# Full-width state products in the first unit of a gated linear-attention kernel, and one output product of the third unit placed in front of the fifth unit's logarithms

## The chip, the cores and the metric

The kernel runs on one core of a Trainium2 chip. The core has a matrix engine (PE, with its weight loads shown as PEld), a vector engine (DVE), a scalar engine (ACT), a general engine (POOL) and an engine that only issues transfers (SP). Each of them works through its own list of instructions in order, and they wait for one another through semaphores. The metric is the device time of one execution in microseconds (us), the median of several runs.

## The reference

A gated recurrence over 4 batches of 8 heads, 768 tokens and head size 48 is followed by a feed-forward block with the ELU function. All in float32:

```python
mag = np.sqrt(a_re * a_re + a_im * a_im)
scale = np.minimum(mag, 0.999) / (mag + 1e-06)
a_re_n, a_im_n = (a_re * scale, a_im * scale)
for t in range(S):
    ar, ai = (a_re_n[:, :, t, :, None], a_im_n[:, :, t, :, None])
    new_re = ar * S_re - ai * S_im
    new_im = ar * S_im + ai * S_re
    kv = np.einsum('bhd,bhe->bhde', k[:, :, t], v[:, :, t])
    S_re, S_im = (new_re + kv, new_im)
    y[:, :, t] = np.einsum('bhd,bhde->bhe', q[:, :, t], S_re)
...
x = np.ascontiguousarray(attn_out.transpose(0, 2, 1, 3)).reshape(B * S, H * D)
h = x @ w_in
g = np.where(h > 0.0, h, alpha * (np.exp(np.minimum(h, 0.0)) - 1.0))
return (g @ w_out).astype(np.float32)
```

The feed-forward block has 3072 tokens, width 384 and inner width 2048.

## The kernel before

**Units.** The work is cut into 12 units, numbered from 0. A unit is one stretch of 128 tokens of two sequences (two of the four batches), so 256 tokens. Units 0 and 1 hold the first 128 tokens of the two pairs of sequences, units 2 and 3 the next 128, and so on. Inside a unit the index n picks the sequence, and each stretch of 128 tokens is treated as two chunks of 64 (index c).

**Decays.** The recurrence is unrolled with logarithms and angles. For units 2 and later a unit's chain is: squares of the gate's parts on ACT (`squares`, L709 and L710), their sum (`joined`, L716, on DVE for units 0 to 2 and on POOL after), two logarithms on ACT (`logarithms`, L735 and L736), two exponentials on ACT (`powers`, L746 and L747), then `lengths` (L772, DVE), `ratios` (L759 and L760, POOL), `slopes` (L780, DVE), `angles` (L815, ACT), the sums of logarithms on PE (`quartered`, L883, which reads the result of `lengths`), exponentials (L893, ACT), the sums of angles on PE (`turned`, L832), sines and cosines (`waves`, ACT), and the scaled and gated keys and queries. Squares, logarithms, exponentials and sines lie in different ACT function tables, and a change of table is an instruction of its own.

**Attention of a unit.** `transposed` turns the gated keys and queries (L1003, copied out of PSUM by ACT at L1004). `scores` makes the 64x64 products inside each chunk (L1011), masked by DVE at L1016. `states` multiplies gated keys and values into the state's increment (L1035) and DVE updates the state S (L1044 where there is no state yet, else L1046, then L1048). `values` makes the outputs from scores (L1058) and from the state (L1065); ACT copies them out (L1073, L1077), and `seam` moves some rows by DMA (L1090) so that they form the input x of the feed-forward block.

In `states` the 128 rows of a stretch are two chunks of 64 rows, each with its own accumulator tile g. The gated keys of a head have two parts (real and imaginary, index i), each padded from 48 to 64 columns:

```python
        for h in range(H):
            for c, g in enumerate(gs):
                for i in range(2):
                    nc.tensor.matmul(
                        g[ts(i, HP), h], lhsT=gates["k"][ts(c, L), n, h, i],
                        rhs=vn[u % 2][ts(c, L), n, ts(h, D)], start=True, stop=True,
                    )
```

So each of these products uses a 64x64 quarter of the PE array: 8 heads x 2 chunks x 2 parts = 32 products for one n.

**Feed-forward of a unit.** `inner` multiplies x with w_in (L1110), `elu` applies the function (ACT L1119 and L1120, DVE L1121) into g. For units 0 and 1 `project` multiplies with w_out (L1131). From unit 2 on the second product is made as a Winograd-like scheme of seven products of half size: DVE forms sums and differences of g (`folded`, L1194) and of w_out (`combined`, L1174, once), and `product(u, k, h)` for k = 1 to 7 and two halves h multiplies them (L1216). `product(u, 1, 1)` ends with an ACT copy of the first product (L1224) into a tile named ee; `product(u, 6, ...)` writes the other half of the same PSUM tile. DVE and ACT finish the outputs (L1228, L1235, L1237, L1241), and SP stores them (L1238).

**Order.** Nothing schedules these steps for the kernel: the order in which the steps are called is the order of each engine's instructions. A list written out by hand, `first` (L1352 to L1411), comes first; it also holds the conversion of the weights from 64-bit to 32-bit floats (`convert`, DVE L40 to L50 and L653), cut into pieces between the other steps. All later steps are put in a plan with a due time each (`put`, `decays_of`, `gates_of`, `values_of`, `layer_of`, L1412 to L1436), and those that are not in `first` already follow in the order of their due times:

```python
    items = [(fn, tuple(args)) for fn, *args in first]
    items += [x[2:] for x in sorted(plan, key=lambda x: x[:2]) if x[2:] not in items]
```

Of the kernel before, what the change touches and what calls it, by code (L numbers as in the profile page):

```python
# [17 lines left out]
L = 64  # L18
# [50 lines left out]
HP = 64  # L69
# [436 lines left out]
def kernel(  # L506
# [13 lines left out]
    B, H, S, D = q.shape  # L520
# [38 lines left out]
    vn = [cst.tile([C, NB, HD + G], FP32, name=f"vn{n}") for n in range(2)]  # L559
    gates = {key: cst.tile([C, NB, H, 2, HP], FP32, name=key + "g") for key in ("k", "q")}  # L560
# [10 lines left out]
    def work(shape, tag="w"):  # L571
        return ps.tile(shape, FP32, tag=tag, bufs=3, name=tag)
# [4 lines left out]
    def where(u):  # L577
        return u % (B // NB) * NB, u // (B // NB) * C
# [114 lines left out]
    def new(tag, bufs=1, shape=None):  # L693
        return sb.tile(shape or [C, NB, H, D], FP32, tag=tag, bufs=bufs, name=tag)
# [325 lines left out]
    def states(u, n):  # L1020

        x = nat[u]
        b, s = where(u)
        x["S", n] = [state.get(b + n)]
        if s == S - C:
            last = C // L - 1
        else:
            last = C // L
        gs = [
            work([C, H, D], "w" if u else "mlp") for c in range(last)  # L1030
        ]
        for h in range(H):
            for c, g in enumerate(gs):
                for i in range(2):
                    nc.tensor.matmul(  # L1035
                        g[ts(i, HP), h], lhsT=gates["k"][ts(c, L), n, h, i],
                        rhs=vn[u % 2][ts(c, L), n, ts(h, D)], start=True, stop=True,
                    )
        for c, g in enumerate(gs):
            old = x["S", n][-1]  # L1040
            new_s = new("S", 8, [C, H, D])
            wide = x["T"][:, n, c].unsqueeze(2).to_broadcast([C, H, D])
            if old is None:
                nc.vector.tensor_tensor(out=new_s, in0=g, in1=wide, op=ALU.mult)  # L1044
            else:
                nc.vector.tensor_tensor(out=new_s, in0=g, in1=old, op=ALU.add)  # L1046
                eng = nc.vector if u < 2 else nc.gpsimd
                eng.tensor_tensor(out=new_s, in0=new_s, in1=wide, op=ALU.mult)  # L1048
            x["S", n].append(new_s)
        state[b + n] = x["S", n][-1]  # L1050
# [253 lines left out]
    parts = [("in", m) for m in range(NF // 2)] + [("out", m) for m in range(NF // WF)]  # L1304
# [39 lines left out]
    def values_of(u, *at):  # L1344
        fns = (transposed, "q"), (transposed, "k"), (scores,), (states,), (values,)
        for n in range(NB):
            for x, (fn, *key) in zip(at[5 * n :], fns):
                put(x, fn, u, *key, n)
        put(at[-1], seam, u)
# [14 lines left out]
        (transposed, 0, "k", 0), (transposed, 0, "q", 1), (carry_on, 0), (transposed, 0, "q", 0),  # L1364
        *4 * [(convert,)], (scores, 0, 0), (transposed, 0, "k", 1), (scores, 0, 1), (load_a, 1),
        (squares, 1), (joined, 1), (fetch, "in", 3), (logarithms, 1), (states, 0, 0),
        (values, 0, 0), (powers, 1), (convert,), (states, 0, 1), (lengths, 1), (load_qk, 1),
        (convert,), (ratios, 1), (values, 0, 1), (seam, 0), (warm, 2), (warm, 2), (decays, 1),
        (load_a, 2), (warm, 1), (inner, 0, 0), *2 * [(convert,)], (noted, 1), (scaled, 1),
# [37 lines left out]
        (scores, 3, 0), (inner, 2, 8), (elu, 2, 6), (combined, 3, 0), (inner, 2, 10), (noted, 3),  # L1407
        (elu, 2, 8), (elu, 2, 10), (combined, 3, 1), (transposed, 3, "q", 1), (values, 3, 0),
        (inner, 2, 12), (transposed, 3, "k", 1), (states, 3, 1), (elu, 2, 12), (scores, 3, 1),
        (inner, 2, 14), (elu, 2, 14), (values, 3, 1), (folded, 2, 0),  # L1410
    ]  # L1411
    def layer_of(u, at_h, at_p):  # L1412
        for m in range(NF // 2):
# [64 lines left out]
```

## Time and profile before

| what | value |
|---|---|
| median of 5 runs | 705.52 us |
| the five runs | 702.76, 704.08, 705.52, 705.54, 705.6 us |
| the profiled execution, device time | 703.02 us |
| its span, first to last instruction | 701.3 us |
| PE busy | 671.9 us (96%), 6720 matmul records |
| PE weight loads busy | 577.4 us (82%) |
| DVE, ACT, POOL busy | 388.7, 398.9, 197.5 us |
| mean granted PE clock | 0.991 of full speed |
| instruction queue of PE (q8) | 55 packets, 0.90 MB |

Times in the profile are microseconds from the start of the span. A product in float32 appears as two weight loads and two matmul records. In a line of the timeline, the numbers are start and length in us, then the engine, the line of the kernel, the operation, what is written and read, and how many records were merged; a bracket gives the idle time of the engine just before, and what ended it. In a line of the waits, the numbers are total us, times and the longest. Lengths of matmul records overlap, since matmuls are pipelined.

### The profile page before, as it was taken

The numbers are of one execution on the slowest core, as the hardware profiler recorded it, in microseconds if no ns is written. First come the engines' busy times: TensorE is split into PE (matmuls) and PEld (weight loads), VectorE is DVE, ScalarE is ACT, GpSimd is POOL, SyncE is SP. The second block draws the span as 40 slices with busy tenths as digits, with TensorE's granted clock in tenths as the row PEclk, the third lists the DMA queues.
The fourth block names the chain that finished last, engine by engine and source line by source line (L and its number), as shares of the span: only waits on it lengthen the run. The fifth ranks groups of instructions, "written<-read, shape, count | busy, mean of one in ns | idle before, by whom it ended". The sixth has DMA issues, their size and how long they took to land.

```text
span 701.3 us, 15900 instructions
## 1 busy us (share of the span) xinstructions
PE 671.9 (96%) x6720; PEld 577.4 (82%) x6720; DVE 388.7 (55%) x579; ACT 398.9 (57%) x630; POOL 197.5 (28%) x207
## 2 busy tenths in 40 slices
PE   8798899988998999999999999999999999999996
PEld 6677776566787888888988989889888988989995
DVE  5989999713955554554553553553554643642151
ACT  6865445658563765755656656657557547641230
POOL 2000000125413414415415405405407305402000
PEclk9999999999999999999999999999999999999999
DMA  9976646062062821921821831731741531100001
GB/s 165 188 146 109 152 140 175 6 110 53 5 133 63 134 51 41 141 41 52 125 60 53 122 60 53 113 70 53 109 74 53 113 70 53 47 1 7 23 0 29
DMA packets 149900, 56.00 MB, mean 80 GB/s; under 512 B 129172, under 2 KB 142652, under 8 KB 149820
## 3 DMA queue, kind: packets, MB, share of 16 engines
q1 hardware_dynamic: 146240, 53.53, 39.9%
q0 software_dynamic: 3360, 1.22, 1.4%
q8 instruction: 55, 0.90, 0.6%
q14 instruction: 25, 0.20, 0.1%
q10 hardware_dynamic: 220, 0.14, 0.1%
HBM read 48.88 MB, written 4.78 MB: 77 GB/s over the span
## 4 chain that ended last, share of the span: by engine, by line
PE 81%; DVE 6%; SPq 3%; DMA 3%; ACT 3%; issue 2%; POOL 1%; DVEq 0%; ACTq 0%; POOLq 0%
PE mlp L1110 30%; PE mlp L1216 26%; PE w L1003 5%; PE mlp L1131 4%; PE w L1011 3%; PE w L1035 3%; PE y L1065 3%; SPq L596 2%; PE y L1058 2%; DMA w<-in_moe_w_in_dram 2%; PE w L832 2%; PE w L1131 1%; PE w L883 1%; DVE wf L43 1%; DVE g L1121 1%
## 5 line engine op out<-in xcount | busy, mean ns | idle before, releaser
L1110 PE MATMUL mlp<-x,w_in 128*128 128x256 f32 x1152 | 261.9, 381 | 2.3 <-DVE g L1121 1.0
L1110 PEld LDWEIGHTS mlp<-x,w_in 128*128 128x128 f32 x1152 | 214.4, 190 | 32.4 <-DVE g L1121 1.8
L1119 ACT ACTIVATE ee<-mlp 128x512 f32<-128x512 f32 x96 | 57.3, 597 | 129.9 <-PE mlp L1110 120.4
L1121 DVE SCALAR_TENSOR_TENSOR g<-ee,mlp 128x512 f32<-128x512 f32 x96 | 65.4, 684 | 118.0 <-ACT ee L1120 110.7
L1216 PE MATMUL mlp<-w_out,g 128*128 128x192 f32 x640 | 111.3, 328 | 0.0
L1216 PEld LDWEIGHTS mlp<-w_out,g 128*128 128x128 f32 x640 | 104.3, 190 | 2.8
L1048 POOL TENSOR_TENSOR S<-S,T 128x384 f32<-128x384 f32 x36 | 29.8, 829 | 165.6 <-DVE S L1046 165.6
L1120 ACT ACTIVATE ee<-ee 128x512 f32<-128x512 f32 x96 | 60.5, 631 | 2.8
L1216 PE MATMUL mlp<-w,g 128*128 128x192 f32 x320 | 58.0, 337 | 2.9 <-ACT ee L1224 2.9
L1216 PEld LDWEIGHTS mlp<-w,g 128*128 128x128 f32 x320 | 52.6, 193 | 8.8 <-issue 5.0
L1194 DVE TENSOR_TENSOR g<-g 128x512 f32<-128x512 f32 x80 | 56.8, 710 | 2.7
L856 POOL DMA_DIRECT2D carry<-n x10 | 5.0, 499 | 144.7 <-DVE n L840 144.7
L1046 DVE TENSOR_TENSOR S<-w,S 128x384 f32<-128x384 f32 x38 | 21.1, 555 | 40.8 <-PE w L1035 25.5
L988 POOL TENSOR_TENSOR kg<-k,cs 128x1536 f32<-128x1536 f32 x9 | 38.9, 4322 | 16.3 <-issue 16.3
L1090 POOL DMA_DIRECT2D x<-y x65 | 31.7, 495 | 41.6 <-ACT y L1077 41.6
L893 ACT ACTIVATE n<-w 64x384 f32<-64x384 f32 (+1 forms) x60 | 28.1, 486 | 26.8 <-PE w L883 26.1
L1235 ACT COPY o<-mlp 128x192 f32<-128x192 f32 x10 | 3.2, 318 | 62.8 <-DMA out_dram<-o 52.9
L716 POOL TENSOR_TENSOR n<-n 128x768 f32<-128x768 f32 x9 | 16.3, 1816 | 66.9 <-ACT n L710 66.9
L1131 PE MATMUL mlp<-w_out,g 128*128 128x384 f32 x96 | 32.9, 490 | 1.6 <-DVE g L1121 1.6
L1004 ACT COPY qt<-w 128x512 f32<-128x512 f32 x48 | 25.4, 584 | 12.0 <-PE w L1003 12.0
L1011 PEld LDWEIGHTS w<-qt,kt 128*64 128x64 f32 x768 | 24.5, 137 | 7.9 <-issue 4.5
L1216 PE MATMUL mlp<-wt,g 128*128 128x192 f32 x160 | 30.1, 331 | 0.0
(165 smaller groups left out, 977.4 us busy)
## 6 DMA issues: line engine op xcount, KB each, us to landing
w<-in_moe_w_out_dram SPq DMA_DIRECT2D x8, 768.0 KB
g<-in_moe_w_in_dram SPq DMA_DIRECT2D x16, 384.0 KB
g<-in_moe_w_out_dram SPq DMA_DIRECT2D x16, 384.0 KB
w<-in_moe_w_in_dram SPq DMA_DIRECT2D x16, 288.0 KB
vn<-in_v_dram SPq DMA_DIRECT2D x24, 192.0 KB
out_dram<-o SPq DMA_DIRECT2D x48, 96.0 KB
ar<-in_a_re_dram SPq DMA_DIRECT2D x22, 192.0 KB
ai<-in_a_im_dram SPq DMA_DIRECT2D x22, 192.0 KB
```

Source lines behind the costliest of these rows:

```text
L988: eng.tensor_tensor(out=to[:, :, :, 0:D], in0=each.unsqueeze(2).to_broadcast([C, step * H, 2, D]), in1=x["cs"][:, n * H : (n + step) * H], ...
L1003: nc.tensor.transpose(t[:, h], of, ident)
L1011: nc.tensor.matmul(t[ts(c, L), h], lhsT=x["kt", n][:, h, ts(c, L)], rhs=x["qt", n][:, h, ts(c, L)], start=True, stop=True,)
L1048: eng.tensor_tensor(out=new_s, in0=new_s, in1=wide, op=ALU.mult)
L1090: eng.dma_start(out=x["x"][ds(j * HP + D, G), i], in_=x["y"][ds(j * HP + i * G, G)])
L1110: nc.tensor.matmul(t[:, e], lhsT=w_in[:, i, ts(f + e, C)], rhs=x["x"][:, i], start=(i == 0), stop=(i == NI - 1),)
L1119: nc.scalar.activation(out=e, in_=t, func=AF.Relu, scale=-1.0)
L1120: nc.scalar.activation(out=e, in_=e, func=AF.Exp, scale=-1.0)
L1121: nc.vector.scalar_tensor_tensor(out=x["g", f // 8][:, f % 8 : f % 8 + 2], in0=e, scalar=-1.0, in1=t, op0=ALU.add, op1=ALU.max)
L1131: nc.tensor.matmul(x["o", n], lhsT=x["g", f // 8][:, f % 8, ts(n, C)], rhs=w_out[:, f], start=(f == 0), stop=(f == NF - 1),)
L1194: nc.vector.tensor_tensor(out=S_of(u, k, h), in0=a, in1=b, op=op)
L1216: nc.tensor.matmul(to, lhsT=a[:, m], rhs=b[:, m], start=(first and h == 0 and m == 0), stop=False, skip_group_check=True,)
```

## The change

In `states`, for unit 0 only, the two parts of a head's keys are taken as one weight of 128 columns, and the product writes all 128 partitions of the accumulator at once. All other units keep the two parts. In the list `first`, eight entries are added, among them `(product, 2, 1, 1)`, directly behind `(product, 2, 1, 0)` and in front of `(product, 2, 4, 0)`, `(logarithms, 4)` and `(powers, 4)`.

```diff
         for h in range(H):
             for c, g in enumerate(gs):
-                for i in range(2):
+                k = gates["k"][ts(c, L), n, h]
+                parts = [(g[ts(i, HP), h], k[:, i]) for i in range(2)]
+                if u == 0:
+                    parts = [(g[:, h], k.rearrange("p i d -> p (i d)"))]
+                for to, of in parts:
                     nc.tensor.matmul(
-                        g[ts(i, HP), h], lhsT=gates["k"][ts(c, L), n, h, i],
-                        rhs=vn[u % 2][ts(c, L), n, ts(h, D)], start=True, stop=True,
+                        to, lhsT=of, rhs=vn[u % 2][ts(c, L), n, ts(h, D)], start=True, stop=True,
                     )
...
-        (inner, 2, 14), (elu, 2, 14), (values, 3, 1), (folded, 2, 0),
+        (load_a, 4), (inner, 2, 14), (elu, 2, 14), (values, 3, 1), (folded, 2, 0),
+        (begun, 4), (squares, 4), (joined, 4), (product, 2, 1, 0), (product, 2, 1, 1),
+        (product, 2, 4, 0), (logarithms, 4), (powers, 4),
```

In the instruction lists of the two kernels this comes to three differences. On PE, the two groups of 32 products 64x48 of unit 0 become two groups of 16 products 128x48. On PE, the 16 products that followed `values` of unit 3 stood as 4 of k=1, 4 of k=4, 4 of k=1, 4 of k=4 and now stand as 8 of k=1 and 8 of k=4. On ACT, the copy L1224 of unit 2 stood behind the two logarithms and the two exponentials of unit 4 with their two table changes, and now stands behind the two squares and in front of the first table change. The lists of DVE, POOL and SP are the same in both, so no transfer moves.

## The prediction

> **What bounds the kernel.** The page comes first: PE is busy for 671.9 of 701.3 us, and in the chain of work that ended last it holds 81%. So a change counts where PE stands still, or where something else sets PE's pace. The waits of PE from 110 us on name the largest stop:
>
> ```profile
> engine line waited for: us in total, times, longest us
> PE mlp L1216 <- ACT ee L1224: 2.9, 1, 2.9
> PE w L1003 <- POOL kg L988: 1.4, 1, 1.4
> PE w L883 <- DVE n L772: 1.3, 1, 1.3
> ```
>
> It occurs once, in the place of the second edit. The timeline of ACT there shows why:
>
> ```profile
> 205.42 0.84 ACT L710 ACTIVATE n<-ai 128x768 f32<-128x768 f32 x1
> 206.28 1.28 ACT L735 ACT_TABLE_LOAD   x1
> 207.57 0.84 ACT L735 ACTIVATE n<-ar 128x768 f32<-128x768 f32 x1
> 208.32 0.83 ACT L736 ACTIVATE n<-n 128x768 f32<-128x768 f32 x1
> 209.17 1.28 ACT L746 ACT_TABLE_LOAD   x1
> 210.46 0.94 ACT L746 ACTIVATE n<-n,ln_eps 128x768 f32<-128x768 f32 x1
> 211.31 0.83 ACT L747 ACTIVATE n<-n 128x768 f32<-128x768 f32 x1
> 212.04 0.30 ACT L1224 COPY ee<-mlp 128x192 f32<-128x192 f32 x1
> ```
>
> The copy of 0.30 us stands behind 5.8 us of other work, and PE, done with its 16 products at 209.49 (208.03 + 1.46), stays idle until 212.39. The table of stretches shows a second cost: the granted clock (the column after POOL) halves behind the stop.
>
> ```profile
> 210.00:212.00 2.00, 0.00 (x0) 0.00 (x0) 1.93 (x5) 1.99 (x3) 0.00 (x0) 1.00 0.00 0
> 212.00:214.00 2.00, 1.61 (x9) 1.61 (x10) 0.83 (x1) 0.34 (x2) 1.79 (x1) 0.95 0.34 82
> 214.00:216.00 2.00, 2.00 (x7) 2.00 (x7) 0.00 (x0) 0.00 (x0) 1.92 (x2) 0.50 0.36 122
> 216.00:218.00 2.00, 2.00 (x12) 0.72 (x12) 1.35 (x3) 0.25 (x1) 2.00 (x5) 0.70 0.05 11
> ```
>
> The trace's clock record puts the half speed at 213.80 to 217.22. The 16 records of product 6 take 4.15 us there; 16 like them at 217.62 take 2.87.
>
> For the first edit, the chain of waits up to 104 us runs mostly over DVE, which converts weights, so what counts there is what makes DVE late. PE and DVE in unit 0:
>
> ```profile
> 33.54 0.65 PE L1065 MATMUL y<-qt,S 128*48 128x64 f32 x16 [1.23 <-DVE S L1044]
> 34.13 0.78 PE L1035 MATMUL mlp<-vn,kg 64*64 64x48 f32 x34
> 36.24 0.97 PE L1035 MATMUL mlp<-vn,kg 64*64 64x48 f32 x28 [1.34 <-issue]
> 37.23 0.56 DVE L1044 TENSOR_TENSOR S<-mlp,T 128x384 f32<-128x384 f32 x1 [1.62 <-PE mlp L1035]
> ```
>
> PE stops for 1.34 us amid the second group of state products with nothing to wait for, and DVE waits 1.62 us for it. Behind it the clock is halved again, 36.30 to 39.72.
>
> **Edit 1, the stop.** The instruction queue q8 brings PE's list in packets of 16384 bytes, 55 for its 13,440 loads and matmuls with their semaphores: 256 instructions each. One packet runs from 33.54 to 34.86, and PE goes on 1.38 us after its end, at instruction 705 counted from the start. The other stop marked "issue" (1.02 us, until 72.81) ends 1.48 us after packet 69.77 to 71.33. So both are late instructions. Here a rule speaks otherwise: the Trainium skill, "Runtime: NRT & Kernel Launch", Instruction fetch mechanics, has the same 256-instruction blocks but calls crossing one mostly hidden. By it the stop would be something else and could remain, and this edit would gain 0.3 us at most. I follow the row. A product is 4 instructions, so the edit drops 2 x 16 x 4 = 128, half a block. Instruction 705 then lies just inside the second L1065 group, which cannot start before 36.7 (below). A packet asked for at most 0.7 us later, because the first group runs longer, still frees PE by 36.95.
>
> **Edit 1, the price.** In the trace the starts of the quarter-array products repeat every 58.5 ns for four records. Their weight load of 64 columns lasts 135 ns, one of 128 columns (L1110) 190 ns: 55 ns more. The full-width slot, two records side by side on the two row halves, is estimated as 58.5 + 55 = 113 ns. No row shows such a product; below, the slot cannot be under 58.5 ns, above it is 190 + 218 = 408 ns if load and matmul don't overlap at all. I take 113, since loads overlap matmuls in every row here. A group has 16 slots either way: 16 x 113 ns = 1.81 us plus the 0.21 us by which the old one (1.15 us) exceeds 16 x 58.5 ns: 2.02 us, 0.87 more. The skill's rule against this edit is "TensorE: Matmul & The Clock Gate", Part 3 (small K and small M: combine row and column tiles). By the rule alone two groups lose 2 x 0.87 = 1.74 us; by the rows most of that is covered:
>
> - First group: 30.69 + 2.02 = 32.71. DVE can't take it before 32.94 (it is in L716, which waited for ACT and a DMA). Cost 0, margin 0.23.
> - Second group: 34.13 + 2.02 = 36.15 instead of 37.2. DVE's L1044 moves from 37.23 to 36.15: **1.08 us gained**. With slots of 58.5 ns it would be 1.6 (L653 ends at 35.61).
> - Seam: L1065 starts at 36.75, ends by 37.6; ACT's copies follow L747, which ends at 37.88 anyway, so x is there 1.4 us earlier. DVE is late next.
>
> DVE has no idle over 0.5 us from 39 to 79, and then waits for a weight DMA whose issue itself waited for DVE, so the 1.08 us should pass on to PE at 104.
>
> **Edit 2.** Of what moves, four products, their records and one ACT copy are all; no DMA and nothing on SP, POOL or DVE.
> - Both halves of product 1 end near 206.9 (204.03 plus 16 records of 2.87). Their second half reads g, ready at 204.46. The copy runs 206.9 to 207.2, so the first table change starts 0.95 us late, and all behind it on ACT too: L746 ends at 212.35, not 211.40.
> - PE's product 4 ends at 209.5, product 6 follows without a stop, to 212.3. Its second half needs the seventh L1194 (204.37 + 7 x 0.89 = 210.6), and starts at 210.9.
> - **The new wait:** L883 needs L772, which needs L746: 212.4 to 213.35. PE idles 1.1 us before L883, and all its later work is queued behind. L883 starts at 213.40, not 216.47. At full clock it takes 0.88 us, as at 166.28, not 1.22. So it ends at 214.28, not 217.69: **3.4 us gained**.
> - Is the clock whole? The window 210.39 to 213.80 would hold some 2.3 us of PE work. The one at 101.2 to 104.6 with 1.82 us was followed by full clock, the one with 1.41 us was not.
> - Covers: POOL's L759 and L760 start 0.95 late and end at 217.3, DVE's L780 at 218.3, and the arctangent, behind L893 and a table change, comes at 218.5: margin 0.2. L832 had 0.47 us in hand. The POOL-issued seam DMAs land by about 222 for a use at 226. Each costs only its overshoot.
>
> **Sum.** 1.08 + 3.41 = 4.5 us. On the profiled execution: 703.02 - 4.5 = 698.5. That execution lies 2.5 us under the median, and the trace doesn't tell why; two earlier stops lie near the edge where the clock halves, and the window's place may differ from run to run. I take the gain from the median: 705.52 - 4.5 = **701.0 us**.
>
> **Rivals.**
> - *The clock halves anyway behind the 1.1 us stop at L883.* A half-speed window of 3.41 us costs up to 1.7: 702.7. For it: the edge lies unknown between 1.41 and 1.82 us of work. Chance 0.13.
> - *No gain in unit 0*: the block lands as late as before, or a fixed transfer holds DVE: 702.1. For it: DMA at full share (1.14) there; against it: DVE's only long wait is for its own releases. 0.14.
> - *The row halves take turns*: slot twice 113 ns, group 3.8 us. The second group then ends near 31.9 + 2 x 3.8 = 39.5 (31.9 is 30.69 with 1.2 us for L1044 and L1065 between the groups), DVE loses 2.3 us: 704.4, no change. Against it: 32 records on one row half (units 10 and 11) and 64 on both halves take the same 1.06 and 1.08 us. 0.06.
> - *Slower: loads and matmuls of full-width products don't overlap.* Place: both L1035 groups of unit 0, at 408 ns a slot and 6.5 us a group. By the same sum DVE's L1044 comes near 44.9, 7.7 us late; less 3.4: 709.8. It decides from 4.4 us a group (31.9 + 2 x 4.4 = 37.2 + 3.4). 0.07.
>
> **Numbers.** My case has 0.60. Within 0.3% (2.1 us, what this measurement can tell) means 703.4 to 707.6. Faster 0.78 (my case and most of the first two rivals), same 0.15, slower 0.07. The range runs from the profiled execution's base with the short slot (703.02 - 5.0 = 698.0) to the near edge of the taking-turns case, 704.0; my case alone is 698.5 to 702.5.
>
> **What would show it.** The wait of L1216 for L1224 is gone, and one of L883 for L772 of about 1.1 us is new; L1224 runs near 206; clock 1.00 there. In unit 0, 32 records in about 2.0 us a group, no issue stop, DVE's L1044 wait near 0.5. I am wrong if the groups take over 4 us, if the clock still halves, or if DVE gives the 1.1 us back at a DMA before 104.

## The result and the profile after

The changed kernel takes 701.16 us, median of 25 runs (697.8 to 705.22); the kernel before, run beside it and now 46 times, 704.87 us (700.23 to 708.14). The ratio is 0.9952, with a 95% interval of 0.9939 to 0.9966: 3.4 us less, between 2.4 and 4.3; the two medians differ by 3.7. The profiled execution took 701.45 us, with a span of 699.7 us.

The longest of the waits of PE from 110 us on (total us, times, longest) in the changed kernel; L1219 and L1227 are the former L1216 and L1224, since the lines of the changed kernel stand 3 further down from `states` on (4 at the state products, now L1039):

```profile
PE w L883 <- DVE n L772: 2.4, 2, 1.3
...
```

The wait of 2.9 us for the copy is gone. The wait of L883 for L772, which stood once at 1.3 us, now stands twice with 2.4 in all, so the new one has 1.1 us. PE's timeline in that place, first in the kernel before:

```profile
202.37 0.69 PE L1058 MATMUL y<-a,vn 64*64 64x64 f32 x32
...
212.39 4.15 PE L1216 MATMUL mlp<-w,g 128*128 128x192 f32 x16 [2.90 <-ACT ee L1224]
216.47 1.22 PE L883 MATMUL w<-n,sum_logs 64*64 64x384 f32 x8
```

and in the changed kernel:

```profile
204.74 0.69 PE L1061 MATMUL y<-a,vn 64*64 64x64 f32 x32
...
206.39 2.87 PE L1219 MATMUL mlp<-w_out,g 128*128 128x192 f32 x16
209.10 2.76 PE L1219 MATMUL mlp<-wt,g 128*128 128x192 f32 x16
211.70 3.08 PE L1219 MATMUL mlp<-w,g 128*128 128x192 f32 x16
215.89 0.88 PE L883 MATMUL w<-n,sum_logs 64*64 64x384 f32 x8 [1.12 <-DVE n L772]
```

Products 1, 4 and 6 follow each other without a stop, and product 6 takes 3.08 us instead of 4.15. ACT's timeline shows the copy where the second edit put it, waiting 0.67 us for PE, and the first table change behind it:

```profile
207.79 0.84 ACT L710 ACTIVATE n<-ai 128x768 f32<-128x768 f32 x1
209.30 0.32 ACT L1227 COPY ee<-mlp 128x192 f32<-128x192 f32 x1 [0.67 <-PE mlp L1219]
209.63 1.28 ACT L735 ACT_TABLE_LOAD   x1
```

From L1058 (now L1061) of unit 3 to L883 of unit 4 it was 216.47 - 202.37 = 14.10 us; it is 215.89 - 204.74 = 11.15 us. But this place lies 2.4 us later in the execution than before. Unit 0 shows where that starts:

```profile
34.25 0.65 PE L1068 MATMUL y<-qt,S 128*48 128x64 f32 x16 [1.51 <-DVE S L1047]
34.83 2.43 PE L1039 MATMUL mlp<-vn,kg 64*128 64x48 f32 x32
```

The stop without a cause is gone and the second group has 32 records. But it starts 0.7 us later than before, because a load of unit 1 landed later (ACT's L710, which waits for it, starts at 31.89 instead of 31.19), and it takes 2.43 us. The table of stretches (the clock is the number behind POOL) of the changed kernel shows the reason for the latter:

```profile
36.00:38.00 2.00, 2.00 (x45) 1.91 (x46) 0.92 (x3) 1.99 (x3) 0.00 (x0) 0.55 0.65 124
38.00:40.00 2.00, 2.00 (x32) 1.74 (x28) 1.97 (x4) 1.18 (x3) 0.00 (x0) 0.50 0.47 95
```

Half speed holds from 36.21 to 43.04, where it ended at 39.72 before, and once more from 49.86 to 53.28. PE starts its first output product (L1131 before, L1134 now) at 105.98 instead of 103.98. So in this pair of executions the second edit gives all of the gain, and PE has lost 2 us by its first output product. Whether that loss is the first edit's doing, and whether it occurs in the timed runs, is the question of the experiments.

### The profile page after: what moved, and what is told of

It reads as the page before. It is cut to its first block, busy times and chain, and to the rows that moved or that the text cites. A ratio compares the mean times of both kernels' runs of the same rounds, so it can differ in the third digit from the quotient of the medians.

```text
span 699.7 us, 15771 instructions
## 1 busy us (share of the span) xinstructions
PE 674.0 (96%) x6656; PEld 580.3 (83%) x6656; DVE 389.1 (56%) x579; ACT 398.3 (57%) x630; POOL 196.9 (28%) x207
## 4 chain that ended last, share of the span: by engine, by line
PE 83%; DVE 5%; SPq 3%; ACT 3%; DMA 2%; issue 2%; POOL 1%; ACTq 0%; POOLq 0%; DVEq 0%
PE mlp L1113 33%; PE mlp L1219 26%; PE w L1003 5%; PE y L1068 3%; PE w L1011 3%; PE w L1039 3%; SPq L596 2%; PE y L1061 2%; PE mlp L1134 2%; PE w L832 2%; PE w L883 1%; DMA w<-in_moe_w_out_dram 1%; DMA w<-in_moe_w_in_dram 1%; DVE wf L43 1%; PE w L1134 1%
## 5 line engine op out<-in xcount | busy, mean ns | idle before, releaser
L1219 PE MATMUL mlp<-w_out,g 128*128 128x192 f32 x640 | 111.1, 328 | 0.0
L1219 PEld LDWEIGHTS mlp<-w_out,g 128*128 128x128 f32 x640 | 104.3, 190 | 2.8
L1219 PE MATMUL mlp<-w,g 128*128 128x192 f32 x320 | 56.9, 332 | 0.0
L1219 PEld LDWEIGHTS mlp<-w,g 128*128 128x128 f32 x320 | 51.6, 190 | 5.8 <-issue 4.8
L716 POOL TENSOR_TENSOR n<-n 128x768 f32<-128x768 f32 x9 | 16.3, 1816 | 66.9 <-ACT n L710 66.9
L1134 PE MATMUL mlp<-w_out,g 128*128 128x384 f32 x96 | 32.9, 490 | 0.8 <-DVE g L1124 0.8
L988 DVE TENSOR_TENSOR qg<-q,cs 128x1536 f32<-128x1536 f32 (+1 forms) x12 | 19.5, 1622 | 19.7 <-ACT cs L966 19.7
```

The source lines that it names most:

```text
L988: eng.tensor_tensor(out=to[:, :, :, 0:D], in0=each.unsqueeze(2).to_broadcast([C, step * H, 2, D]), in1=x["cs"][:, n * H : (n + step) * H], ...
L1134: nc.tensor.matmul(x["o", n], lhsT=x["g", f // 8][:, f % 8, ts(n, C)], rhs=w_out[:, f], start=(f == 0), stop=(f == NF - 1),)
L1219: nc.tensor.matmul(to, lhsT=a[:, m], rhs=b[:, m], start=(first and h == 0 and m == 0), stop=False, skip_group_check=True,)
```

## The experiments

All ratios are to runs of the kernel before on the same chip. Four kernels take the two edits apart.

**Edit 1 alone**: the changed kernel with the list `first` as before.

```diff
-        (load_a, 4), (inner, 2, 14), (elu, 2, 14), (values, 3, 1), (folded, 2, 0),
-        (begun, 4), (squares, 4), (joined, 4), (product, 2, 1, 0), (product, 2, 1, 1),
-        (product, 2, 4, 0), (logarithms, 4), (powers, 4),
+        (inner, 2, 14), (elu, 2, 14), (values, 3, 1), (folded, 2, 0),
```

> The changed kernel without the second edit: full-width state products in unit 0, the order of the products of unit 2 and the logarithms of unit 4 as before. My sum as predicted: 1.08 us under the kernel before (ratio 0.9985), no stop marked issue in the second group of state products. The theory formed from the profile of the changed kernel: the stop is gone, but the clock stays halved for longer behind the slow groups, so that this edit brings 0 to 0.4 us (ratio 0.9995 to 1.000). A rival, that the edit costs time (slots without overlap), would give 704.5 us or more over the same base: ratio over 1.002. In all cases PE's 2.9 us wait for the copy L1224 stays, and the clock halves behind it.

Measured: 702.71 us against 704.25, ratio 0.9986 (0.9963 to 1.0009): 1.0 us less, with an interval from 2.6 less to 0.6 more. The size agrees with the sum's 1.08; no change is not excluded. Its profile shows where the stop went (PE's timeline):

```profile
35.71 1.99 PE L1039 MATMUL mlp<-vn,kg 64*128 64x48 f32 x32
37.63 0.69 PE L1061 MATMUL y<-a,vn 64*64 64x64 f32 x32
38.34 0.31 PE L1068 MATMUL y<-qt,S 128*48 128x64 f32 x2
39.14 1.09 PE L1068 MATMUL y<-qt,S 128*48 128x64 f32 x14 [0.49 <-issue]
```

It has moved two records into the second y products, where the count of 128 instructions puts it, and is 0.49 us long. The second group takes 1.99 us at full clock. The wait for the copy and the half clock behind it are there as before: product 6 takes 4.19 us.

**Edit 2 alone**: the kernel before, with quarter-array products in all units, and the new list.

```diff
-        (inner, 2, 14), (elu, 2, 14), (values, 3, 1), (folded, 2, 0),
+        (load_a, 4), (inner, 2, 14), (elu, 2, 14), (values, 3, 1), (folded, 2, 0),
+        (begun, 4), (squares, 4), (joined, 4), (product, 2, 1, 0), (product, 2, 1, 1),
+        (product, 2, 4, 0), (logarithms, 4), (powers, 4),
```

> The kernel before with the second edit alone: quarter-array state products everywhere, both halves of product 1 and its copy in front of the logarithms of unit 4. If the second edit is worth what was predicted: 3.4 us under the kernel before, ratio 0.9952, no wait of PE for the copy L1224, a new wait of L883 for L772 of 1.1 us, full clock there. The 1.34 us stop of unit 0 stays. A rival, that unit 0 brings the larger part: ratio 0.997 or more.

Measured: 701.71 us against 704.25, ratio 0.9967 (0.9948 to 0.9987): 2.3 us less, between 0.9 and 3.7. The predicted 3.4 lies inside. In its profile L883 of unit 4 starts at 212.44, 11.15 us after L1058 of unit 3 at 201.29, to the hundredth what the changed kernel shows:

```profile
201.29 0.69 PE L1058 MATMUL y<-a,vn 64*64 64x64 f32 x32
...
212.44 0.88 PE L883 MATMUL w<-n,sum_logs 64*64 64x384 f32 x8 [1.12 <-DVE n L772]
```

The two edits alone add to 1.0 + 2.3 = 3.3 us, close to the 3.4 that both give together; each of the two is uncertain by about 1.5 us.

**The full-width product in all units**, the price without cover:

```diff
-                if u == 0:
+                if True:
```

> The changed kernel with full-width state products in all units, not only in unit 0: the price of the full-width product where PE sets the pace and nothing covers it. Estimate of 113 ns a slot: 0.87 us more in each of the 18 groups of units 1 to 9, and about 0.8 in each of the 4 groups of units 10 and 11, which have one chunk: 19 us more than the changed kernel, ratio to before near 1.022. If full-width products took no longer a slot than quarter-array ones (58.5 ns): no change against the changed kernel. If load and matmul don't overlap (408 ns a slot): 110 us more.

Measured, in two runs: 720.31 us, ratio 1.0228 (1.0178 to 1.0278). That is 19.2 us over the changed kernel, where 19 were worked out from slots of 113 ns. One group of unit 4 in its timeline takes 1.92 us from its start to that of the next product, where quarter-array products took 1.08 (263.05 - 261.97). The kernel before and this one:

```profile
261.97 1.15 PE L1035 MATMUL w<-vn,kg 64*64 64x48 f32 x64
263.05 1.57 PE L1216 MATMUL mlp<-w_out,g 128*128 128x192 f32 x8
...
266.59 1.99 PE L1039 MATMUL w<-vn,kg 64*128 64x48 f32 x32
268.51 1.57 PE L1219 MATMUL mlp<-w_out,g 128*128 128x192 f32 x8
```

So both rivals on the price fall (row halves in turn, no overlap of loads), and where nothing covers the group, the packing rule that the prediction set against this edit is right by nearly a factor of two (1.92 against 1.08).

**The first group alone** full-width, with edit 2:

```diff
-                if u == 0:
+                if u == 0 and n == 0:
```

> The changed kernel with full-width products only in the first group of unit 0 (n = 0); the second group keeps quarter-array products. PE's list is then 64 instructions shorter than before, not 128, so the end of the instruction block should fall 64 instructions later, at the start of the y products behind the second group. If late instructions are the cause of the stop: no stop inside the second group, which takes 1.15 us again, and at most a stop of 0.5 us in front of the y products; DVE's L1044 of the second group waits under 0.5 us. If the stop is tied to the second group itself and not to the place in the list, it stays inside the group. Time: 0.5 to 0.9 us under the changed kernel if the longer second group costs what its 0.87 us suggest (ratio to before 0.994), equal to it if unit 0 is covered.

 

> Full-width products in the first group of unit 0 alone, with the second edit, once more: is it faster than the changed kernel on the same chip? If the longer second group is uncovered, 0.5 to 0.9 us faster. If the later end of the instruction block (two records into the y products) costs as much as the shorter group saves, equal within 0.3%.

Measured: 698.75 us, ratio 0.9932 (0.991 to 0.9954), and on another chip 699.73 us, ratio 0.9944 (0.9921 to 0.9967). PE's list is 64 instructions shorter than before here. The timeline of its first run:

```profile
34.88 1.15 PE L1039 MATMUL mlp<-vn,kg 64*64 64x48 f32 x64
35.85 0.29 PE L1061 MATMUL y<-a,vn 64*64 64x64 f32 x2
38.43 0.69 PE L1061 MATMUL y<-a,vn 64*64 64x64 f32 x30 [2.30 <-issue]
```

The stop stands exactly 64 instructions further on, at the start of the y products, and no longer inside the second group. So it belongs to a place in PE's list and not to these products: in all seven profiles that show it, of six kernels, exactly 348 matmul records stand ahead of it. The expected length (0.5 us at most) was wrong: it is 2.30 us, and 1.69 in the second run, because the packet of instructions came later: it ran from 35.66 to 37.04. DVE, though, no longer waits for the group. Its L1047 came at 36.28, without idle time ahead of it.

The next kernels concern the clock and the loss of PE by its first output product.

**The changed kernel again.**

> The changed kernel once more, beside the next three on one chip, for a second profile. If the 2.0 us that unit 0 lost in its first profile come from when the first loads land and from where the clock's windows fall, this profile shows another place and number of half-clock windows before 110 us, while the full-width groups take 1.99 us at full clock. If the loss belongs to the edit, PE reaches its first output product again 2 us later than in the kernel before (near 106.0). Ratio to before near 0.995 in both cases.

Measured: 701.65 us, ratio 0.9963 (0.9942 to 0.9985). The group takes 1.99 us at full clock, and the half-clock windows lie elsewhere: 21.18 to 28.01, 48.49 to 51.90, 79.21 to 82.62. PE nevertheless reaches its first output product at 106.23. So the first reading (where the windows fall) and the second (the loss belongs to the edit) each got one of their two signs. But the half-speed time ahead of that product is the same in both profiles, 13.7 us, where the kernel before has 6.8.

**PE kept busy in the wait of the kernel before**: 12 idle products in front of product 6, the order as before.

```diff
+        if u == 2 and k == 6 and h == 0:
+            t = work([C, C])
+            for _ in range(12):
+                nc.tensor.matmul(t, lhsT=ident, rhs=ident, start=True, stop=True)
```

> The kernel before, with 12 idle products of 128x128 (24 records, 2.6 us at full clock) put into PE's 2.9 us wait for the copy L1224; they compute nothing that is used, and the order of the products and the logarithms stays that of before. If the wait alone costs, nothing changes: L883 starts 14.1 us after the y products L1058 of unit 3, as before (216.47 less 202.37). If the half clock behind the wait is a cost of its own, it is gone: product 6 takes 2.9 us instead of 4.15, and L883 starts about 1.3 us earlier, 12.8 us after L1058, and takes 0.88 us instead of 1.22. Ratio to before 0.9975 to 0.999.

Measured: 703.14 us, ratio 0.9988 (0.9967 to 1.0009). By the time alone that is no change. The profile decides:

```profile
202.56 0.69 PE L1058 MATMUL y<-a,vn 64*64 64x64 f32 x32
...
209.52 2.84 PE L1218 MATMUL w<-ident 128*128 128x128 f32 x24
212.58 2.87 PE L1220 MATMUL mlp<-w,g 128*128 128x192 f32 x16 [0.22 <-ACT ee L1228]
215.38 0.88 PE L883 MATMUL w<-n,sum_logs 64*64 64x384 f32 x8
```

With PE doing work that nobody uses, the clock stays whole in this execution, product 6 takes 2.87 us instead of 4.15, and L883 comes 12.82 us after L1058 instead of 14.10. So 1.3 us of what the second edit gains up to L883 are the half clock and not the wait itself, and another 0.34 fall on L883. The other profile that has the wait, that of edit 1 alone, shows the half clock behind it too (216.64 to 220.05); none of the ten others does.

**PE filled in unit 0**: 6 idle products in its wait between the first y products and the second group, in the changed kernel (twice), and with the first group alone.

```diff
+        if u == 0 and n == 0:
+            warm(6)
         for p, c, j in each:
             if x["S", n][c] is not None:
```

> The changed kernel with 6 idle products of 128x128 (12 records, about 1.3 us at full clock) in PE's wait between the first y products and the first state products of unit 0; they compute nothing that is used. They lengthen PE's list by 24 instructions. If PE's idle time there is what halves the clock near 36 us, that window is at full clock now and unit 0 gains 0.5 to 1.5 us over the changed kernel. If the slow full-width groups themselves count as too little work, the clock halves there all the same and the time stays.

 

> The changed kernel with the 6 idle products in PE's first wait of unit 0, once more, since its ratio of 0.9933 lies beside 0.9952 and 0.9963 of the changed kernel with intervals that touch. If the filling helps: near 0.993 again. If it was chance: near 0.995 to 0.996.

 

> Both at once: full-width products in the first group of unit 0 alone, and the 6 idle products in PE's wait behind it, with the second edit. PE's list is 40 instructions shorter than before, so the end of the instruction block should fall 24 instructions earlier than with the first group alone: inside the second group, some 10 records before its end, instead of two records into the y products. If that is so, DVE waits for the second group again, by over 1 us, and the version is no faster than the first group alone (0.9932 and 0.9944). If the two add up: near 0.992.

Measured: 699.72 us, ratio 0.9933 (0.991 to 0.9957), and 700.61 us, ratio 0.9953 (0.9932 to 0.9974); with the first group alone 698.76 us, ratio 0.9932 (0.9905 to 0.9959). None of the three profiles has a half-clock window near 36 us. But neither has the second one of the changed kernel, without any filling, and the two filled runs differ as much from each other as from the changed kernel (0.9952 and 0.9963). The times alone show no effect of the filling. The clock of the timed runs hints at one: its median is 0.994 and 0.993 in the filled runs (8 and 11), and 0.989 in both sets of the changed kernel (27 and 12). The filling also makes PE's list 24 instructions longer, so what raised the clock is not shown. In the third the stop was expected inside the second group with over 1 us of wait on DVE; DVE waited 0.30 us, since the packet happened to end at 34.41. Where the block ends is set by the list, but what the stop costs is set by when the packet comes.

## Why the prediction was right, and the term that was too large

Predicted were 701.0 us and a gain of 4.5; measured are 701.16 and 3.4 (2.4 to 4.3 by the ratio; 3.7 by the medians). The mechanism held for the second edit, and for the cause of the stop and the price in the first; that the first edit's gain reaches PE at 104 is not borne out by the profiles.

- **Edit 2, the wait and its successor: right.** The copy comes 2.91 us after the first product, as the 2.87 of the sum had it; L883 waits 1.12 us (1.1). To L883's start the profiles give 2.95 us (3.07 expected), to its end 3.29 (3.41). The difference of 0.12 us is mostly that L883 starts 0.15 us after the end of L772, where the sum had 0.05. Product 6 took 3.08 us where 2.87 were taken, but that lies inside the wait.
- **Edit 2, the half clock: right,** by the kernel that keeps PE busy. The timed 2.3 us (0.9 to 3.7) lie under the profiled 3.29. The half-clock part of 1.6 us need not occur in every execution of the kernel before, since the windows fall elsewhere in each; it did occur in both profiles that have the wait. That is argued, not shown; the clock of the timed runs fits it (median 0.9885 with edit 2 alone, 0.986 before).
- **Edit 2, the covers: held.** L780 starts at 219.33 and the arctangent, which was to have 0.2 us in hand, at 220.99, 0.7 after the end of L780.
- **Edit 1, the cause of the stop: right,** where the Trainium skill ("Runtime: NRT & Kernel Launch", Instruction fetch mechanics) calls the crossing of a block mostly hidden; here it cost up to 2.30 us. The stop moved by the count of instructions dropped, not with the products.
- **Edit 1, the price: right.** 1.99 us a group for 2.02, and 19.2 us for 19 in all units.
- **Edit 1, the cover of the first group: thin.** The margin of 0.23 us is used up where unit 1's load lands earlier relative to PE: in the profile of edit 1 alone DVE waits 0.22 us for the first group.
- **Edit 1, the 1.08 us on DVE: held, with a stop of that length.** From DVE's first update of the state in unit 0 (L1044, now L1047) to the second it was 37.23 - 32.94 = 4.29 us. In the three profiles with the new unit 0 and no filling it is 3.65 (the changed kernel), 3.20 (again) and 3.22 (edit 1 alone): 0.6 to 1.1 less. But edit 2 alone, with the old groups, has 3.22 as well, since its stop lasted only 0.61 us. The sum took the stop's length from one execution.
- **Edit 1, the 1.08 us that "should pass on to PE at 104": the step that the profiles do not bear out.** PE's first output product starts at 103.98, 102.93 and 104.21 in the three profiles with the old unit 0 (before, edit 2 alone, kept busy), and at 105.98, 106.87 and 106.23 in the three with the new one and no filling (changed, edit 1 alone, changed again): some 2.7 us later on the mean, not 1.1 earlier. What lies in between is half clock. Ahead of that product the old three have 6.8, 6.8 and 10.2 us at half speed, the new three 13.7, 20.5 and 13.7. In all three new ones a window falls at 48 to 53 us, and behind it DVE waits for the sums of angles, as here in the changed kernel run again:

```profile
53.53 0.56 DVE L837 TENSOR_SCALAR rnd<-w 128x384 f32<-128x384 f32 x1 [1.41 <-PE w L832]
```

None of the old three profiles has either. Nor have the two filled profiles, though both their groups are full-width: from DVE's second update to PE's first output product they take 66.9 and 66.8 us, as the old three do (66.0 to 66.8), where the new three take 68.5 to 69.1. So most of the 2 us come with that window and not from the groups' own length. Why a window falls there in some profiles is not shown.

The timed runs do not show this loss: edit 1 alone is 1.0 us faster there, within 1.6. The clock says why the profiles mislead, for the mean granted clock of each timed run is on record. The kernel before has 0.991 in its profile and a median of 0.986 in the timed runs; edit 2 alone 0.994 and 0.9885; kept busy 0.990 and 0.988. These profiles are 1.8, 3.5 and 2.2 us faster than the medians (703.02, 698.21, 700.91 against 704.87, 701.71, 703.14). Edit 1 alone is the other way round: 0.981 in the profile, 0.987 in the timed runs, and 705.71 against 702.71 us. The changed kernel's two profiles are near their medians in both (0.989 and 0.988 against 0.989). So profiles with few half-speed windows were set beside profiles with an ordinary number or many. In the timed runs edit 1 alone has the clock of the kernel before (0.987, 0.986). How much a window costs can be estimated from the 196 runs whose clock is on record (without the kernel with full-width products in all units): a straight line, with an offset for each kernel, gives 0.34 us for each us at half speed, so 1.2 us for a window of 3.41. By this estimate the changed kernel is 1.6 us faster than the one before at equal clock, and the rest of its gain is its higher clock.

The term that was too large is not settled to the tenth: of the 1.1 us missing in the timed total, the pieces that were timed alone put 0.1 in edit 1 and 1.1 in edit 2, each with an interval wider than that. Taking the gain from the median, not from the profiled execution, was right. That 701.0 came within 0.2 us is luck on top: the five runs that it started from have a median of 705.52, 0.65 us above that of the 46, and the gain was too large by 0.8 us (4.5 against 3.7 by the medians). The two errors nearly cancel.

The version with only the first group full-width and the second edit was measured at 0.9932 and 0.9944. That is under the changed kernel's 0.9952 and 0.9963 in both of its comparisons, by about 1.4 us, with intervals that overlap. Its timed runs also have the higher clock (median 0.994 and 0.992 against 0.989). It keeps the half of the edit that is covered and drops the half that isn't; it is likely the better kernel, not certainly so.

## What to carry to other kernels

A short copy in an in-order list costs what stands in front of it: look where the engine that reads its result, or the tile under it, stands still, and move the copy in front of the longer work even if that work then starts later, after following the delay to its first reader. A stop with no releaser on PE can be its own instruction list arriving late; counting instructions from the stop tells where it goes when the list gets shorter, and a costlier but shorter form of some products can pay only where other work covers it. A gap on PE costs twice when the clock halves behind it, and the second part can be measured with idle products in the gap. One profile is one execution: before two profiles are compared for a difference of a few us, the clock of each is compared with that of its kernel's timed runs.

## What the runs showed of the hardware

- **When PE runs out of instructions, it goes on 1.4 to 1.6 us after the packet ends.** Packet end and restart: 34.86 and 36.24 (before), 34.18 and 35.63 (edit 2 alone), 37.61 and 39.14 (edit 1 alone), 37.04 and 38.43 (first group alone), 35.73 and 37.16 (kept busy). The same packet started between 32.88 and 36.22 in the runs, while the DMA engines were full (share 1.14 from 32 to 36 us in the kernel before).
- **The half clock comes in windows of 3.41 us or multiples, and its place is a matter of the execution.** In unit 0 it began at times from 18.66 to 21.18 us, and the later windows of an execution begin whole multiples of 3.41 us after it. The Trainium skill ("TensorE: Matmul & The Clock Gate", Part 1) calls the window free-running; the runs agree.
- **A window can be followed by half clock although PE is shown as busy almost throughout.** In the second run of the changed kernel (clock behind POOL):

```profile
45.07:48.48 3.41, 3.13 (x42) 2.81 (x42) 2.87 (x6) 3.05 (x6) 0.00 (x0) 1.00 0.76 136
48.48:51.90 3.42, 3.42 (x9) 2.67 (x10) 3.35 (x6) 1.97 (x2) 0.00 (x0) 0.50 0.95 209
```

The prediction counted 1.41 and 1.82 us of busy time as the two sides of an edge. Here a window with 3.13 us is followed by half clock, where the one with 1.82 us was followed by full clock: no edge in busy time alone fits both. Half of the busy time in the first line is L935, 32 records with two moving columns each, 1.60 us. That such short products count as less work is a guess that no run tests.
